# Scores and states of a pair in one TensorE run, fewer loads in flight, last rows in three parts: a retention layer with an MLP mixer

## The chip, the cores and the metric

The kernel runs on one core of a Trainium2 chip. The metric is the device time of one execution in microseconds (us); the time of a kernel is the median of its runs. Names in this text: PE is TensorE, PEld its weight loads, DVE is VectorE, ACT is ScalarE, POOL is GpSimd, SP is SyncE, whose queue issues most DMAs of the later part. A "line" such as L423 is a line of the kernel before, as the profile gives it.

## The reference

Four batches (B), eight heads (H), 768 steps (S), head width 64 (D). The first part is a recurrent retention layer, the second an MLP mixer over its output with 512 channels.

```python
def _attn_ref(q, k, v):
    gamma = 1.0 - 2.0 ** (-5.0 - np.arange(H))
    scale = 1.0 / np.sqrt(D)
    for t in range(S):
        state = gamma[None, :, None, None] * state + np.einsum('bhd,bhe->bhde', k[:, :, t], v[:, :, t])
        y[:, :, t] = scale * np.einsum('bhd,bhde->bhe', q[:, :, t], state)

def _moe_ref(x, w_tok1, w_tok2, w_ch1, w_ch2):      # x: (4, 768, 512), heads side by side
    xt = x.transpose(0, 2, 1)
    h = np.maximum(xt @ w_tok1, 0.0) @ w_tok2       # 768 -> 256 -> 768 along the steps
    u = x + h.transpose(0, 2, 1)
    h2 = np.maximum(u @ w_ch1, 0.0) @ w_ch2         # 512 -> 1536 -> 512 along the channels
    return u + h2
```

Inputs and output are float32; the kernel multiplies in 16-bit floats and adds up in float32.

## The kernel before

The retention layer is computed in six chunks of 128 steps. Two heads are handled together as a pair; a batch has four pairs, here written (b,p) for pair p of batch b. For each pair there is a **front**:

- q, k and v arrive by DMA. k is scaled into 16 bits on DVE (L332), q and v are cast: in batches 0 and 1 by the DMA itself, in batches 2 and 3 on POOL (L313).
- k and q are turned (head width onto partitions): on PE (L348, L352) with a copy out (L360) in batches 0 and 1, by a transposing DMA on SP's queue (L367) in batches 2 and 3.
- **states**: ten matmuls, 64 columns wide, k chunk by v chunk (L381). Each head uses 64 columns of the array. DVE adds the five products up with decay (U, L390 and L393), ACT and DVE write the result as r (L400, L407).
- **scores**: twelve matmuls on 64 rows of the array each (L423), in two halves of three chunks. DVE multiplies them by the causal mask (L436, "am", four a pair).
- **y**: q by state (L457) and masked scores by v (L460), two halves; ACT and DVE scale them into x (L471, L475), POOL casts x (L488).
- The token mixing: L510 (with w_tok1), a relu on ACT (L518), L531 (with w_tok2), an addition on DVE (L538), a cast of u on POOL (L549). u is turned on PE in batch 0 (L562, copied by ACT at L571) and by a transposing DMA in the other batches (L585; the variable `wide` chooses).

For each batch there is a **back**: the channel mixing, ch1 (L618, 384 columns, 96 matmuls a batch) with a relu on ACT (L631), and ch2 (L651, 512 columns, 72 a batch) with an addition on DVE (L660) and a store of 128 rows by SP (L667).

The program has a planner of its own, `arrange()`. Every operation is an `Op` with an engine, a time of occupation, a latency, dependencies and the tile slots that it takes. The planner places operations one by one on the engines by earliest start and priority, and the instructions are then issued in that order; each engine runs its own list strictly in order. Front matmuls go ahead of back matmuls (priority 0 and 1), back matmuls fill the time in between. `GUARD` is added to the planned start of a front matmul of batches 1 to 3, `SEM` stands for a semaphore, `RING` is the number of loads that the planner lets SP and POOL have in flight, `LATE` sets a pair's priority against the others. These numbers act on the order alone; the hardware waits for semaphores.

PSUM has eight banks: five "fa" (all fronts) and three "ba" (back; in batch 0 also the front). The banks of a name go round in order of taking. Before the change, states take one fa bank, each half of the scores two, and the three are separate operations on PE that the planner can put in different places. In batch 0 matmuls on zeros (L210) fill waits of PE.

Of the kernel before, what the change touches and what calls it, by code (L numbers as in the profile page):

```python
# [10 lines left out]
FP = mybir.dt.float32  # L11
# [6 lines left out]
def kernel(  # L18
# [11 lines left out]
    nc = tc.nc  # L30
    B, H, S, D = q.shape
    P = 128
    NC = S // P
    HC = NC // 2
    NP = H // 2
    C = H * D
# [45 lines left out]
    NR = 4  # L82
    r16 = [const_p.tile([P, NC - 1, P], F16, name=f"r16_{i}") for i in range(NR)]
    for t in r16:
# [7 lines left out]


    BUFS = dict(kf=4, qf=4, vf=4, k16=3, q16=4, v16=4, kT=4, qT=4, U=3, am=8, x16=2, h1=4, u16=3, u16w=2,
                x=3, uT=3, h2=2, o=3, r16=NR, fa=5, ba=3)
    SEM, GUARD = 80, 100
    EARLY, LATE, DIRECT = 1000, 12, 3
    LONG, XK, XQ, XU, XBAR = 1, 2, 2, 1, 1200
    RING = dict(SP=3, POOL=6)
    QLONG = 1200  # L100
    ASIDE, RACT = ((1, 1), (1, 3), (2, 1), (2, 3), (3, 1), (3, 3)), ()
    KPOOL = ()
    FREE, FILL, TOKBA, PRE, TWICE, SOFT = 4, 0.75, 2, 2, 1, 2
    ops = []

    class Slot:
# [97 lines left out]
    def tile_of(slot, pool, shape, dtype, tag=None):  # L204
        tag = tag or slot.tag
        slot.tile = pool.tile(shape, dtype, name=tag, bufs=BUFS[tag])
        if pool is ps:

            for _ in range(idle[0]):
                nc.tensor.matmul(slot.tile, zero[:, :P], zero, start=True, stop=True)  # L210
            idle[0] = 0
        return slot.tile
# [21 lines left out]
    def front(b, p):  # L234
# [6 lines left out]

        def op(eng, occ, lat, emit, deps=(), takes=(), uses=()):
            n[0] += 1
            pr = (0 if eng == "PE" else 1, b, n[0] + LATE * p, p)
            o = Op(eng, pr, occ, lat, emit, deps, takes, uses, guard=g if eng == "PE" else 0)
            o.first = p if first else None
            return o
# [79 lines left out]
        def emit():  # L327
            k16 = tile_of(K, sb, [P, NC, 2, D], F16)
            for j in range(2):
                h = 2 * p + j  # L330
                src = KF.tile[:, j * NC:(j + 1) * NC, :]
                (nc.gpsimd if keng == "POOL" else nc.vector).tensor_scalar(  # L332
                    k16[:, :, j, :], src, gk[:, h:h + 1], None, ALU.mult)
# [6 lines left out]
        def turn(src, dst, dep, eng):  # L340
            T = Slot(*FB)

            def emit():
                T.tile = tp = tile_of(T, ps, [P, 512], FP).bitcast(F16)
                for c in range(NC):
                    if src is Q and soft and b < LONG:
                        for j in range(2):
                            nc.tensor.transpose(tp[j * D:(j + 1) * D, c * P:(c + 1) * P],  # L348
                                                src.tile[:, j * NC + c], ident16)
                        continue  # L350
                    o = src.tile[:, c] if src is K else src.tile[:, 2 * c:2 * c + 2]
                    nc.tensor.transpose(tp[:, c * P:(c + 1) * P], o.rearrange("p h d -> p (h d)"), ident16)  # L352
            t = op("PE", 340, 500, emit, [dep, t1_done.get(b * NP - 1) if b > 0 else None], [T], [src])

            def emit():
                d, o = tile_of(dst, sb, [P, S], F16), T.tile[:, :S]
                if dst is QT and b < LONG:
                    d = d.rearrange("d (f p i) -> d f i p", f=2, i=HC)
                    o = o.rearrange("d (f i p) -> d f i p", f=2, i=HC)
                (nc.scalar.copy if eng == "ACT" else nc.vector.tensor_copy)(d, o)  # L360
            occ = dict(ACT=1350 if dst is QT and b < LONG else 700, DVE=470)[eng]
            return op(eng, occ, occ + 90, emit, [t], [dst], [T])
# [11 lines left out]

        ST, US, RS = Slot(*FB), Slot("U"), Slot("r16")

        def emit():
            st = tile_of(ST, ps, [P, 512], FP)
            for c in range(NC - 1):
                for j in range(2):  # L380
                    nc.tensor.matmul(st[j * D:(j + 1) * D, c * D:(c + 1) * D], K.tile[:, c, j],  # L381
                                     V.tile[:, j * NC + c], start=True, stop=True)
        pp = op("PE", 300, 470, emit, [kc, vc, y_done.get(b * NP + p - 2), t1_done.get(b * NP - 1) if b > 0 else None], [ST], [K, V])
        prev = None
        for c in range(NC - 1):
            def emit(c=c):
# [22 lines left out]

        AM = [Slot("am") for _ in range(4)]  # L410
        am_ops = []
        two_before = y_done.get(b * NP + p - 2)
        for hf in range(2):
            A = [Slot(*FB), Slot(*FB)]

            def emit(hf=hf, A=A):
                a = [tile_of(A[j], ps, [P, 512], FP).rearrange("p (i t) -> p i t", t=P)
                     for j in range(2)]
                for i in range(HC):
                    t = slice((hf * HC + i) * P, (hf * HC + i + 1) * P)  # L420
                    for j in range(2):
                        r = slice(j * D, (j + 1) * D)
                        nc.tensor.matmul(a[j][:, i], KT.tile[r, t], QT.tile[r, t],  # L423
                                         start=True, stop=True)
            a = op("PE", 180, 350, emit, [kt, qt, two_before], A, [KT, QT])
            for j in range(2):
                off = first and (p, 2 * hf + j) in ASIDE
                M = AM[2 * hf + j]

                def emit(j=j, A=A, off=off, M=M):  # L430
                    am = tile_of(M, sb, [P, HC, P], F16)
                    src = A[j].tile.rearrange("p (i t) -> p i t", t=P)
                    if off:
                        nc.scalar.copy(am, src[:, :HC])
                    else:
                        nc.vector.tensor_tensor(am, src[:, :HC], mask, ALU.mult)  # L436
                m = op(*(("ACT", 390, 470) if off else ("DVE", 470, 550)), emit, [a], [M], [A[j]])
                if off:
                    def emit(M=M):
                        nc.gpsimd.affine_select(  # L440
                            out=M.tile, in_=M.tile, compare_op=ALU.is_ge, fill=0.0,
                            base=0, pattern=[[0, HC], [1, P]], channel_multiplier=-1)
                    m = op("POOL", 470, 540, emit, [m], [], [M])
                am_ops.append(m)
# [73 lines left out]
            nc.scalar.activation(h1.rearrange("p j c -> p (j c)"), T1.tile[:, :NJ * P], AF.Relu)  # L518
        hr = op("ACT", 300, 380, emit, [t1], [H1], [T1])
        tt, uc = [], None  # L520
        wide = b >= XU
        T, UW = Slot(*FT), Slot("u16w")
        for hf in range(2):
            T2, U16 = Slot(*FT), UW if wide else Slot("u16")
# [73 lines left out]
    def back(b):  # L598
# [37 lines left out]
        def ch2(sh):  # L636
            H2, rel = halves[sh]
            for i in range(HC):

                parts = 2 if (b, sh, i) == (B - 1, 1, HC - 1) else 1  # L640
                CW = C // parts
                for part in range(parts):
                    A, O = Slot("ba"), Slot("o")
                    cs = slice(part * CW, (part + 1) * CW)
                    last = None
                    for f0 in range(0, NF, 2):
                        def emit(f0=f0, i=i, A=A, H2=H2, cs=cs, CW=CW):
                            if f0 == 0:
                                tile_of(A, ps, [P, 512], FP)
                            for ft in range(f0, f0 + 2):  # L650
                                nc.tensor.matmul(A.tile[:, :CW], H2.tile[:, ft, i * P:(i + 1) * P],  # L651
                                                 wc2[:, ft, cs],
                                                 start=(ft == 0), stop=(ft == NF - 1))
                        last = op("PE", 432 // parts, 432 // parts + 170, emit,
                                  rel[f0:f0 + 2] + [wops["c2", 0], last],
                                  [A] if f0 == 0 else [], [H2] if f0 == 0 else [A, H2])

                    def emit(sh=sh, i=i, A=A, O=O, cs=cs, CW=CW):
                        o = tile_of(O, sb, [P, C], FP)
                        nc.vector.tensor_tensor(o[:, :CW], X.tile[:, sh * HC + i, cs], A.tile[:, :CW],  # L660
                                                ALU.add)
                    ad = op("DVE", 80 + CW, 160 + CW, emit,
                            [last] + [x_add[b, p, sh] for p in range(NP)], [O], [A, X])

                    def emit(sh=sh, i=i, O=O, cs=cs, CW=CW):
                        t0 = (sh * HC + i) * P
                        nc.sync.dma_start(out=out[b, t0:t0 + P, cs], in_=O.tile[:, :CW])  # L667
                    st = op("SP", 100, 100, emit, [ad], [], [O])
                    st.prio, st.dma = (-2, b), 800 // parts

        for part in ((ch1, 0), (ch1, 1), (ch2, 0), (ch2, 1)) if b < TWICE else ((ch1, 0), (ch2, 0), (ch1, 1), (ch2, 1)):
            part[0](part[1])
# [52 lines left out]
```

## Time and profile before

| | us |
|---|---|
| median of 7 runs | 201.38 (201.27 to 201.99) |
| the profiled execution | 201.54 |
| its span | 199.8 |
| back matmuls, L618 busy | 69.5 |
| back matmuls, L651 busy | 68.0 |
| masks, L436 busy on DVE | 28.1 |
| relus of ch1, L631 busy on ACT | 46.4 |

The span runs from the first instruction to the last in the profile; the execution's time is a little longer. Matmuls are pipelined: one that is listed with 326 ns can start 163 ns after the one before it. So the distance between starts, not the listed length, tells what PE spends on a matmul. Idle time stands in square brackets behind an instruction, with what ended it.

### The profile page before, as it was taken

To read this page: it belongs to the slowest core of one execution; us is meant where nothing else is said; L and a number is where in the kernel's file an instruction comes from. 1 tells how busy PE (TensorE), PEld (TensorE's weight loads), DVE (VectorE), ACT (ScalarE), POOL (GpSimd) and SP (SyncE) were. 2 spreads that over 40 slices of the span, in tenths; PEclk is the share of its full clock that TensorE was granted. 3 is DMA by queue.
4 is the path that set the end of the run, shared out by engine and by line. 5 is a ranking of instruction groups with operands and counts; after the bars stand their busy time and mean duration, and the time that the engine had idled before them with its cause. 6 is when DMAs were issued, how large, how long until landed. Compare 5 with 4: busy or idle time off the path is not lost.

```text
span 199.8 us, 4681 instructions
## 1 busy us (share of the span) xinstructions
PE 190.2 (95%) x1868; PEld 116.4 (58%) x1868; DVE 112.7 (56%) x285; ACT 92.5 (46%) x207; POOL 76.7 (38%) x124
## 2 busy tenths in 40 slices
PE   7688899999999999999999999999999999999993
PEld 2444696667755664666566745675657545545552
DVE  6498965398568875683969376938481121021021
ACT  7259988886555200553226511563127405504600
POOL 7997999913901450235333504152422100000000
PEclk9999999999999999999999999999999999999999
DMA  6999999999998999999999999999940121012012
GB/s 113 178 216 186 208 228 199 160 190 218 155 95 187 202 246 164 223 250 158 206 204 239 234 171 242 235 206 194 185 122 27 39 86 72 3 52 105 0 52 105
DMA packets 90069, 31.75 MB, mean 159 GB/s; under 512 B 82592, under 2 KB 85920, under 8 KB 90048
## 3 DMA queue, kind: packets, MB, share of 16 engines
q1 hardware_dynamic: 64800, 21.63, 56.0%
q0 software_dynamic: 25248, 9.83, 40.3%
q8 instruction: 14, 0.23, 0.5%
q14 instruction: 7, 0.06, 0.1%
HBM read 26.74 MB, written 6.29 MB: 165 GB/s over the span
## 4 chain that ended last, share of the span: by engine, by line
PE 73%; DMA 10%; POOL 6%; issue 3%; ACT 2%; SPq 2%; DVE 2%; POOLq 0%
PE ba L618 30%; PE ba L651 25%; DMA kf<-in_k_dram 5%; PE fa L531 4%; PE fa L510 4%; DMA vf<-in_v_dram 3%; DMA qf<-in_q_dram 2%; PE fa L423 2%; SPq L367 2%; PE fa L460 2%; PE fa L381 1%; POOL v L301 1%; PE fa L457 1%; PE fa L352 1%; POOL v L313 1%
## 5 line engine op out<-in xcount | busy, mean ns | idle before, releaser
L618 PE MATMUL ba<-uT,wc 128*128 128x384 f16 x384 | 69.5, 326 | 0.0
L651 PE MATMUL ba<-wc,h 128*128 128x512 f16 (+1 forms) x300 | 68.0, 371 | 0.0
L631 ACT ACTIVATE h<-ba 128x384 f16<-128x384 f32 x96 | 46.4, 491 | 35.3 <-PE ba L618 34.5
L618 PEld LDWEIGHTS <-wc 128*128 128x128 f16 x384 | 35.6, 98 | 21.7
L651 PEld LDWEIGHTS <-h 128*128 128x128 f16 x300 | 27.5, 98 | 26.6
L660 DVE TENSOR_TENSOR o<-x,ba 128x512 f32<-128x512 f32 (+1 forms) x25 | 16.6, 665 | 38.6 <-PE ba L651 38.3
L436 DVE TENSOR_TENSOR am<-fa,mask 128x384 f16<-128x384 f32 x55 | 28.1, 550 | 4.1 <-PE fa L423 3.9
L488 POOL CAST x<-x 128x384 f16<-128x384 f32 x30 | 14.9, 509 | 31.2 <-issue 21.0
L538 DVE TENSOR_TENSOR x<-x,fa 128x384 f32<-128x384 f32 x31 | 16.1, 549 | 9.3 <-PE fa L531 8.8
L549 POOL CAST u16w<-x 128x384 f16<-128x384 f32 x24 | 12.0, 514 | 23.7 <-DVE x L538 22.8
L471 ACT ACTIVATE x<-fa,gy 128x192 f32<-128x192 f32 (+1 forms) x34 | 12.5, 422 | 17.7 <-PE fa L460 17.7
L332 DVE TENSOR_SCALAR k<-kf,gk 128x384 f16<-128x384 f32 x32 | 14.4, 493 | 5.4 <-DMA kf<-in_k_dram 5.4
L393 DVE SCALAR_TENSOR_TENSOR U<-U,gp,fa 128x64 f32<-128x64 f32 x56 | 15.5, 278 | 1.3
L518 ACT ACTIVATE h<-fa 128x256 f16<-128x256 f32 x15 | 5.7, 383 | 18.9 <-PE fa L510 15.7
L400 ACT ACTIVATE r<-U 64x320 f16<-64x320 f32 x16 | 7.5, 467 | 14.3 <-DVE U L393 14.2
L460 PEld LDWEIGHTS <-am 128*128 128x128 f16 x192 | 12.2, 98 | 2.2
L531 PE MATMUL fa<-h,wt 128*128 128x128 f16 x186 | 13.2, 219 | 0.0
L531 PEld LDWEIGHTS <-wt 128*128 128x128 f16 x192 | 11.9, 98 | 2.1
L510 PEld LDWEIGHTS <-wt 128*128 128x128 f16 x192 | 11.7, 98 | 2.0
L510 PE MATMUL fa<-x,wt 128*128 128x128 f16 x180 | 12.5, 219 | 0.0
L460 PE MATMUL fa<-v,am 128*128 128x64 f16 x174 | 12.5, 193 | 0.0
L313 POOL CAST q<-qf 128x768 f16<-128x768 f32 x8 | 6.6, 827 | 14.9 <-DMA qf<-in_q_dram 12.4
(74 smaller groups left out, 179.6 us busy)
## 6 DMA issues: line engine op xcount, KB each, us to landing
out_dram<-o SPq DMA_DIRECT2D x23, 256.0 KB, 2.5
kf<-in_k_dram SPq DMA_DIRECT2D x9, 384.0 KB, 5.0
qf<-in_q_dram SPq DMA_DIRECT2D x8, 384.0 KB, 5.0
vf<-in_v_dram SPq DMA_DIRECT2D x8, 384.0 KB, 5.6
kf<-in_k_dram POOLq DMA_DIRECT2D x7, 384.0 KB, 10.3
v<-in_v_dram POOLq DMA_DIRECT2D x8, 192.0 KB, 6.8
wc<-in_moe_w_ch_dram POOLq DMA_DIRECT2D x1, 1536.0 KB, 13.5
wc<-in_moe_w_ch_dram POOLq DMA_DIRECT2D x1, 1024.0 KB, 14.7
```

What stands on the lines that cost most here:

```text
L332: (nc.gpsimd if keng == "POOL" else nc.vector).tensor_scalar(k16[:, :, j, :], src, gk[:, h:h + 1], None, ALU.mult)
L393: nc.vector.scalar_tensor_tensor(U[:, c], U[:, c - 1], gp[:, p:p + 1], o, ALU.mult, ALU.add)
L436: nc.vector.tensor_tensor(am, src[:, :HC], mask, ALU.mult)
L460: nc.tensor.matmul(o[:, j * D:(j + 1) * D], AM[2 * hf + j].tile[:, i], V.tile[:, j * NC + c], start=(c == 0), stop=(c == 0 or j == 1))
L488: nc.gpsimd.tensor_copy(X16.tile[:, half(hf)], X.tile[:, half(hf), pc])
L510: nc.tensor.matmul(acc[:, jt * P:(jt + 1) * P], wt1[:, i, jt * P:(jt + 1) * P], X16.tile[:, i], start=(i == 0), stop=(i == NC - 1))
L531: nc.tensor.matmul(acc[:, i * P:(i + 1) * P], wt2[:, jt, t], H1.tile[:, jt], start=(jt == 0), stop=(jt == NJ - 1))
L538: nc.vector.tensor_tensor(xo, xo, T2.tile[:, :HC * P].rearrange("p (i d) -> p i d", d=P), ALU.add)
L618: nc.tensor.matmul(acc[:, :SH], w[:, ct, f * P:(f + 1) * P], UT.tile[:, ct, sh * SH:(sh + 1) * SH], start=(ct == 0), stop=(ct == NP - 1))
L631: nc.scalar.activation(H2.tile[:, ft], A.tile[:, :SH], AF.Relu)
L651: nc.tensor.matmul(A.tile[:, :CW], H2.tile[:, ft, i * P:(i + 1) * P], wc2[:, ft, cs], start=(ft == 0), stop=(ft == NF - 1))
L660: nc.vector.tensor_tensor(o[:, :CW], X.tile[:, sh * HC + i, cs], A.tile[:, :CW], ALU.add)
```

## The change

Part 1: for batches 1 to 3 (`WHOLE = 1`) the two halves of the scores and the states become one operation on PE, scores first; it takes all five fa banks. Batch 0 keeps the three operations.

Part 2: numbers of the planner. `GUARD` 100 to 150, `RING` of SP 3 to 2, `LATE` for batches 1 to 3 12 to 20, occupation times `AOCC` and `SOCC` for separate scores and states, and `LAG`: a run of batches 2 and 3 depends on the L510 of the second pair of the batch before, no longer of its last pair.

Part 3: u of pair (1,3) is turned on PE (`NOX`), not by a transposing DMA.

Part 4: output tiles 5 in place of 3; the last 128 rows are computed, added and stored in parts of 256, 192 and 64 columns in place of two of 256.

```diff
     BUFS = dict(kf=4, qf=4, vf=4, k16=3, q16=4, v16=4, kT=4, qT=4, U=3, am=8, x16=2, h1=4, u16=3, u16w=2,
-                x=3, uT=3, h2=2, o=3, r16=NR, fa=5, ba=3)
-    SEM, GUARD = 80, 100
+                x=3, uT=3, h2=2, o=5, r16=NR, fa=5, ba=3)
+    SEM, GUARD = 80, 150
...
-    RING = dict(SP=3, POOL=6)
+    RING = dict(SP=2, POOL=6)
...
+    WHOLE, AOCC, SOCC = 1, (370, 520), (360, 500)
+    NOX, LAG = ((1, 3),), 2
...
-            pr = (0 if eng == "PE" else 1, b, n[0] + LATE * p, p)
+            pr = (0 if eng == "PE" else 1, b, n[0] + (LATE if first else 20) * p, p)
...
-            t = op("PE", 340, 500, emit, [dep, t1_done.get(b * NP - 1) if b > 0 else None], [T], [src])
+            t = op("PE", 340, 500, emit, [dep, t1_done.get(b * NP - 1 - LAG * (b > 1)) if b > 0 else None], [T], [src])
...
+        A = [[Slot(*FB), Slot(*FB)] for _ in range(2)]
+        two_before = y_done.get(b * NP + p - 2)
+        whole = b >= WHOLE
...
+        def emit():
+            emit_a(0)
+            emit_a(1)
+            emit_st()
+
+        t1_last = t1_done.get(b * NP - 1 - LAG * (b > 1)) if b > 0 else None
+        if whole:
+            pp = op("PE", 790, 950, emit, [kt, qt, kc, vc, two_before, t1_last], A[0] + A[1] + [ST],
+                    [KT, QT, K, V])
+        else:
+            pp = op("PE", *((300, 470) if first else SOCC), emit_st, [kc, vc, two_before, t1_last], [ST], [K, V])
...
-            a = op("PE", 180, 350, emit, [kt, qt, two_before], A, [KT, QT])
+            a = pp if whole else op("PE", *((180, 350) if first else AOCC), lambda hf=hf: emit_a(hf), [kt, qt, two_before], A[hf], [KT, QT])
...
-        wide = b >= XU
+        wide = b >= XU and (b, p) not in NOX
...
-                parts = 2 if (b, sh, i) == (B - 1, 1, HC - 1) else 1
-                CW = C // parts
-                for part in range(parts):
+                parts = (256, 192, 64) if (b, sh, i) == (B - 1, 1, HC - 1) else (C,)
+                for part, CW in enumerate(parts):
...
-                    st.prio, st.dma = (-2, b), 800 // parts
+                    st.prio, st.dma = (-2, b), 800 * CW // C
```

`emit_a(hf)` and `emit_st()` are the bodies of the old operations: the six score matmuls of half `hf`, and the ten states matmuls.

In the built program this also reorders SP's queue. For batches 2 and 3 the order of loads and transposing DMAs was, in part, `uT(2,0) kT(2,2) qT(2,2) qf(2,3) vf(2,3)`, and later `uT(2,1) ... qT(2,3) kf(3,0) qf(3,0) ... vf(3,0) uT(2,2) kf(3,1) kT(3,0) qT(3,0)`. It becomes `kT(2,2) qT(2,2) qf(2,3) vf(2,3) uT(2,0)` and `qT(2,3) kf(3,0) qf(3,0) ... uT(2,1) kT(3,0) vf(3,0) qT(3,0) kf(3,1) qf(3,1) uT(2,2)` (kf, qf, vf: loads; kT, qT, uT: turned tiles).

More of the change, by code (lines that the diff above doesn't have):

```diff
@@ L375, in front, with emit_st @@
         ST, US, RS = Slot(*FB), Slot("U"), Slot("r16")
-        def emit():
+        A = [[Slot(*FB), Slot(*FB)] for _ in range(2)]
+        two_before = y_done.get(b * NP + p - 2)
+        whole = b >= WHOLE
+        def emit_st():
             st = tile_of(ST, ps, [P, 512], FP)
@@ L382, in emit, with emit_a @@
                                      V.tile[:, j * NC + c], start=True, stop=True)
-        pp = op("PE", 300, 470, emit, [kc, vc, y_done.get(b * NP + p - 2), t1_done.get(b * NP - 1) if b > 0 else None], [ST], [K, V])
+        def emit_a(hf):
+            a = [tile_of(A[hf][j], ps, [P, 512], FP).rearrange("p (i t) -> p i t", t=P)
+                 for j in range(2)]
+            for i in range(HC):
+                t = slice((hf * HC + i) * P, (hf * HC + i + 1) * P)
+                for j in range(2):
+                    r = slice(j * D, (j + 1) * D)
+                    nc.tensor.matmul(a[j][:, i], KT.tile[r, t], QT.tile[r, t], start=True, stop=True)
+        def emit():
[8 more added lines that the diff above has]
+            pp = op("PE", *((300, 470) if first else SOCC), emit_st, [kc, vc, two_before, t1_last], [ST], [K, V])
         prev = None
@@ L411, in front @@
         am_ops = []
-        two_before = y_done.get(b * NP + p - 2)
         for hf in range(2):
[L414 to L424, printed above, removed]
-            a = op("PE", 180, 350, emit, [kt, qt, two_before], A, [KT, QT])
+            a = pp if whole else op("PE", *((180, 350) if first else AOCC), lambda hf=hf: emit_a(hf), [kt, qt, two_before], A[hf], [KT, QT])
             for j in range(2):
@@ L428, in front, with emit @@
                 M = AM[2 * hf + j]
-                def emit(j=j, A=A, off=off, M=M):
+                def emit(j=j, A=A[hf], off=off, M=M):
                     am = tile_of(M, sb, [P, HC, P], F16)
@@ L436, in emit @@
                         nc.vector.tensor_tensor(am, src[:, :HC], mask, ALU.mult)
-                m = op(*(("ACT", 390, 470) if off else ("DVE", 470, 550)), emit, [a], [M], [A[j]])
+                m = op(*(("ACT", 390, 470) if off else ("DVE", 470, 550)), emit, [a], [M], [A[hf][j]])
                 if off:
@@ L638, in ch2 @@
             for i in range(HC):
-                parts = 2 if (b, sh, i) == (B - 1, 1, HC - 1) else 1
-                CW = C // parts
-                for part in range(parts):
+                parts = (256, 192, 64) if (b, sh, i) == (B - 1, 1, HC - 1) else (C,)
+                for part, CW in enumerate(parts):
                     A, O = Slot("ba"), Slot("o")
-                    cs = slice(part * CW, (part + 1) * CW)
+                    c0 = sum(parts[:part])
+                    cs = slice(c0, c0 + CW)
                     last = None
@@ L653, in emit @@
                                                  start=(ft == 0), stop=(ft == NF - 1))
-                        last = op("PE", 432 // parts, 432 // parts + 170, emit,
+                        last = op("PE", 432 * CW // C, 432 * CW // C + 170, emit,
                                   rel[f0:f0 + 2] + [wops["c2", 0], last],
```

## The prediction

> **What bounds the kernel now.** I read the page first: shares of the engines, the slices, the chain that ended last.
>
> ```profile
> PE 190.2 (95%) x1868; PEld 116.4 (58%) x1868; DVE 112.7 (56%) x285; ACT 92.5 (46%) x207; POOL 76.7 (38%) x124
> ...
> PE   7688899999999999999999999999999999999993
> ...
> PEclk9999999999999999999999999999999999999999
> DMA  6999999999998999999999999999940121012012
> ...
> PE 73%; DMA 10%; POOL 6%; issue 3%; ACT 2%; SPq 2%; DVE 2%; POOLq 0%
> ```
>
> TensorE (PE) is busy for 90% or more of every slice from the sixth to the last but one (a slice is 5.0 us), at full clock; no other engine is above 60%. The DMA row is full up to about 145 us, so late operands are the second possible bound. The profiled execution took 201.54 us, 1.74 us more than its span of 199.8, and 0.16 us more than the median of 201.38. I sum against 201.54 and take 0.16 off at the end.
>
> Next the chain in order of time gives the pitch of undisturbed matmuls:
>
> ```profile
> 157.66 7.77 PE ba L651 x36
> 165.43 7.80 PE ba L618 x48
> ```
>
> So 7.80/48 = 0.1625 us for a 384-column matmul and 7.77/36 = 0.216 us for a 512-column one (0.056 us for 128 columns, from 0.67 us for 12). Against these pitches the timeline of PE shows what the change is about (start, length, line):
>
> ```profile
> 37.45 0.98 PE L618 MATMUL ba<-uT,wc 128*128 128x384 f16 x5
> 38.35 0.35 PE L381 MATMUL fa<-v,k 128*64 128x64 f16 x10
> 38.63 0.50 PE L618 MATMUL ba<-uT,wc 128*128 128x384 f16 x2
> ```
> ```profile
> 39.88 0.51 PE L423 MATMUL fa<-qT,kT 64*128 64x128 f16 x12
> 40.32 0.99 PE L618 MATMUL ba<-uT,wc 128*128 128x384 f16 x5
> ```
>
> Lengths overlap, so starts are what counts. Five L618 matmuls should take 5 x 0.1625 = 0.81 us, but the states (L381) start 0.90 after the first: 0.09 for going in. The states hold PE 38.63 - 38.35 = 0.28. Seven L618 follow, 7 x 0.1625 = 1.14, and the scores (L423) start after 1.25: 0.01 for the first matmul after a small run (it shows 0.336 instead of 0.326) and 0.10 for going in. The scores hold PE 0.44. Where a pair's scores stand in two halves:
>
> ```profile
> 126.17 0.34 PE L423 MATMUL fa<-qT,kT 64*128 64x128 f16 x6
> 126.44 0.51 PE L531 MATMUL fa<-h,wt 128*128 128x128 f16 x6
> 126.88 0.34 PE L423 MATMUL fa<-qT,kT 64*128 64x128 f16 x6
> ```
>
> a half holds 0.27, so six matmuls cost 0.44 - 0.27 = 0.17 and going out 0.27 - 0.17 = 0.10. Such a transition is no idle time for the profile; it hides in "busy".
>
> Last the gaps behind which PE really waited:
>
> ```profile
> 86.75 0.35 PE L381 MATMUL fa<-v,k 128*64 128x64 f16 x10 [0.39 <-POOL v L313]
> 122.68 0.35 PE L381 MATMUL fa<-v,k 128*64 128x64 f16 x10 [0.27 <-POOL v L313]
> ```
>
> Going through all runs after 32 us by starts and pitches, six places are longer than pitch plus transitions: 81.7 (0.14), 86.7 (0.46), 92.5 (0.03), 101.6 (0.22), 117.7 (0.18), 122.7 (0.34): 1.36 us of waiting, most of it for the cast of v or a turned q. Everything else on PE after 32 us is work and transitions.
>
> **The change part by part.** I write (b,p) for pair p of batch b. In the changed program PE's order is the same up to the transposes of (1,0) at 37 us, so nothing moves before that.
>
> Scores and states in one run, 12 pairs. Before, an unsplit pair costs 0.09 + 0.28 + 0.01 + 0.10 + 0.44 + 0.01 = 0.93. After: 0.10 in, 0.44 scores, x for the seam from scores to states, 0.28 states, 0.01. The 0.44 already holds a going out of 0.10. This seam is not in the trace; its reverse is, in batch 0:
>
> ```profile
> 8.53 0.35 PE L381 MATMUL fa<-v,k 128*64 128x64 f16 x10 [1.07 <-DMA v<-in_v_dram]
> 8.80 0.34 PE L423 MATMUL fa<-qT,kT 64*128 64x128 f16 x6
> ```
>
> States straight before scores hold 0.27 to 0.28, as they do before a full-width matmul: one going out, no going in beside it. I take the same for the seam, x = 0: after = 0.83, saved 0.10 a pair, 1.20 for twelve. Bounds: nothing is drained (x = -0.10, 2.40 in all) and out plus in are both paid (x = +0.09, 0.12 in all). Three pairs, (1,1), (1,3), (3,1), stand in halves before; each pays one more in and out, 0.10 + 0.10 + 0.01, together 0.63. Sum: -1.83, between -0.75 and -3.03.
>
> The Trainium skill, "TensorEngine Tiling (Array Packing)", section Key Properties, says that changing the tiling mode, not just the tile, drains TensorE. Scores use 64-row, states 64-column tiles, so by that rule "unbroken" still holds one drain: it stands by x = 0, and against a reader's hope of x = -0.10, with which the total below would be 1.2 us lower.
>
> Edits that only steer the planner: AOCC and SOCC are read by no pair (batch 0 keeps the old numbers, all others are whole). GUARD 150 for 100, SP's ring of 2 for 3, 20 for LATE and LAG (the runs of batches 2 and 3 wait for the L510 of two pairs earlier than before) move work but add no instruction. Their price is what becomes of the 1.36 us of waits: from -1.36 (all gone) to the rival below. The six waits would each shrink by at most 0.05 through the larger guard, 0.3 in all; I take -0.15. Output tiles 5 for 3: nothing waited for them (VectorE's output additions, L660, waited for PE), cost 0.
>
> The run takes all five "fa" banks, so the next user (L510, L531 or y) waits for the first mask (L436). After the scores at 83.11 the first mask started at 83.48 and took 0.55: a bank is free 0.92 after the run's start. The nearest follower in the changed order is L510 of (2,0), 1.87 us behind the start of the run of (2,1): covered, price 0. Were VectorE just then in a k scaling (L332, 0.93 for two), the cover would be gone and cost 0 to 0.1.
>
> The u of (1,3) is turned on PE: six 128-column transposes, 6 x 0.056 = +0.34 us on the path. Its copy on ScalarE (700 ns class; L360's copy of the same 128x768 has a pitch of 0.70) lies beside PE; ScalarE is at 46%. If its cover went, ch1 of batch 1 would wait up to 0.7. One transposing DMA leaves SP's queue.
>
> Last rows in three parts: the 512 columns are the same, twelve more matmuls at about 0.0025 us of fixed time each (0.1625 - 384/2400) = +0.03. If a 64-column matmul cannot run under 0.038 (a y triple L457, L460, L460 takes 0.115 with three weight loads), +0.13. Behind the last matmul:
>
> ```profile
> 196.64 0.42 DVE L660 TENSOR_TENSOR o<-x,ba 128x256 f32<-128x256 f32 x1 [0.89 <-PE ba L651]
> ```
> ```profile
> out_dram<-o SPq DMA_DIRECT2D x1, 128.0 KB, 1.7
> ```
>
> The 512-column addition has a mean of 0.686, so a column costs (0.686 - 0.42)/256 = 1.0 ns and 64 columns take 0.42 - 0.20 = 0.22. But SP is now busy: the 192-column store is issued 0.36 + 0.05 after its matmuls, which end 12 x 0.029 = 0.35 before the last; two SP issues stood at least 0.47 apart (60.45, 60.92). So the last issue comes at 0.41 + 0.47 - 0.35 = 0.53 after the last matmul, against 0.49 now. Landing: 2.0 for 256 KB, 1.7 for 128 KB, so 32 KB gains at most 0.22. Net -0.1, from -0.2 to +0.2.
>
> "DMA: Bandwidth & Descriptors", section Specifications, gives 512 B as the smallest transfer at line rate and a read-modify-write below; 64 columns are rows of 256 B. No store here shows it; by that rule the last landing gains nothing and the sum is about 0.1 higher.
>
> Sum: -1.83 - 0.15 + 0.34 + 0.03 - 0.10 = -1.71. 201.54 - 1.71 = 199.83, less 0.16: **199.7 us**.
>
> **Rivals.**
>
> Late operands (slower). A run now needs k, v, both turned tiles and all five "fa" banks at once, and PE is in order: all matmuls behind it wait, and with them ScalarE's relus, y, and the stores on SP. Adding the pitches along the changed PE order, the runs of batches 2 and 3 are due at 77.4, 85.8, 93.8, 102.9, 111.5, 124.9, 136.6, 141.3 us. The turned q landed before at 76.4, 82.9, 96.5, 106.1, 117.6, 124.3, 135.6, 145.5. Four would be late, (3,0) by 6.1 us. For a better landing speaks SP's new order: the turned k and q of (2,2) go ahead of uT of (2,0), which had held SP 2.8 us at 88.7; the turned k and q of (3,0) go ahead of uT of (2,2), which held it 2.65 us at 107.8, and of the next k load, and uT of (2,1) (1.25 us) goes behind the loads of (3,0). Taking just these 2.65 + 1.25 off, q of (3,0) lands at 113.7, 2.2 us late. Price 2.2: 199.7 + 2.2 = 201.9. It decides from 1.7 us of added waiting, a landing after 113.2. Against it: v and the turned tiles were at most 0.46 us late before though the DMA row was full, and the new order moves back-half matmuls ahead of the runs as it needs. (3,1) is tightest on VectorE: 4.6 us from run to y, for four masks at a pitch of 0.47, five U steps of 0.3, one r of 0.51: 3.9.
>
> Both drains paid, that is, the run is not unbroken for PE: -0.75 - 0.15 + 0.27 = -0.63, 200.8. For it: shapes differ on both sides of the seam. Against it: the reverse seam paid one.
>
> No drain at the seam: 1.2 more, 198.5. Against it: states before scores held as long as before L618.
>
> **How the numbers follow.** Forecast 0.54 (199.0 to 200.6), no drain 0.12, both drains 0.12, late operands 0.22. A measurement of this kernel can tell about 0.2%, 0.4 us, from no change. Below 200.98 lie the forecast but for 0.03, no drain and half of both drains: 0.54 - 0.03 + 0.12 + 0.06 = 0.69, rounded with the low end of late operands to 0.70. Above 201.78 lies most of late operands, 0.20, same is 0.10. Range 198.2 (no drain and 0.3 less waiting) to 202.0.
>
> **What would show it.** In the profile of the changed kernel: scores to states 0.44 (forecast), 0.34 (no drain) or 0.53 (both); 0.28 from the first states matmul to the next; PE waits after 32 us of some 1.2 us in sum; the last store issued about 0.5 us after the last matmul. Wrong, if a run at 94, 103, 112 or 141 us stands behind a gap released by a turned tile or by L313, or if y (L457, L460) waits for VectorE.

## The result and the profile after

The changed kernel took 200.11 us in the median of 27 runs, the kernel before 201.30 us in 64 runs beside it: ratio 0.9933, 95% interval 0.9917 to 0.9949. That is 1.35 us less at 201.3, against a forecast of 1.7. The ratio is taken without the few executions in a slower state, so it is not the quotient of the two medians, 0.9941. Single runs reach from 198.23 to 201.97, so only ratios with their intervals are compared below.

The profiled execution took 200.47 us (its span is 198.8), 1.07 less than the profiled execution before. Its page (shares of the engines, the slices of PE and DMA, the chain that ended last):

```profile
PE 189.4 (95%) x1886; PEld 117.4 (59%) x1886; DVE 108.9 (55%) x286; ACT 93.6 (47%) x208; POOL 77.2 (39%) x124
...
PE   7887999999999999999996999999999999999993
...
DMA  6999999999599999999998999999921131012013
...
PE 75%; DMA 10%; POOL 4%; DVE 3%; SPq 2%; ACT 2%; issue 1%; POOLq 0%; DVEq 0%
```

The picture is the same, PE at 95%, but the 22nd slice of PE (104.4 to 109.3 us) is now at 6 tenths. All waits of PE after 32 us that the view of waits names:

```profile
PE fa L524 <- DVE am L450: 1.5, 1, 1.5
PE fa L387 <- DVE x L489: 0.3, 1, 0.3
```

(Engine, line and releaser: total us, times, longest. Line numbers of the changed kernel: scores L397, states L387, masks L450, k scaling L334, scaling of y L489, the two matmuls of the token mixing L524 and L545, ch1 L632, ch2 L665.) The two waits for the cast of v that this view named before (0.39 and 0.27) are gone.

The first unbroken run, in the timeline of PE (start, length):

```profile
38.61 0.81 PE L632 MATMUL ba<-uT,wc 128*128 128x384 f16 x4
39.36 0.51 PE L397 MATMUL fa<-qT,kT 64*128 64x128 f16 x12
39.80 0.35 PE L387 MATMUL fa<-v,k 128*64 128x64 f16 x10
40.08 0.82 PE L632 MATMUL ba<-uT,wc 128*128 128x384 f16 x4
```

Four ch1 matmuls should take 0.65 and the scores start after 0.75: 0.10 for going in. Scores to states 0.44, states to ch1 0.28. Scores held 0.44 before a full-width matmul too, so the seam costs one going out and saves one going in, x = 0 of the prediction. All twelve runs read so, between 0.438 and 0.439, but for one that waits inside (0.80, below). The drain that the Trainium skill, "TensorEngine Tiling (Array Packing)", section Key Properties, states for a change of mode fits this direction as well: 0.44 in place of 0.34.

The hole in it, first on PE, then on VectorE, where the cause is to be seen:

```profile
103.12 0.51 PE L397 MATMUL fa<-qT,kT 64*128 64x128 f16 x12
103.56 0.35 PE L387 MATMUL fa<-v,k 128*64 128x64 f16 x10
103.84 1.47 PE L632 MATMUL ba<-uT,wc 128*128 128x384 f16 x8
106.84 0.27 PE L524 MATMUL fa<-x,wt 128*128 128x128 f16 x2 [1.53 <-DVE am L450]
```

```profile
105.35 0.75 DVE L334 TENSOR_SCALAR k<-kf,gk 128x384 f16<-128x384 f32 x2 [2.86 <-DMA kf<-in_k_dram]
106.01 0.22 DVE L416 COPY U<-fa 128x64 f32<-128x64 f32 x1
106.15 0.55 DVE L450 TENSOR_TENSOR am<-fa,mask 128x384 f16<-128x384 f32 x1
```

The run of (2,3) is done at 103.8 and its masks could start. But VectorE's list has the k scaling of (3,0) ahead of them, and that waits until 105.35 for its load (landed at 105.32). The run holds all five fa banks, the first mask frees the first of them, and L524 of (2,2) needs it: PE stands for 1.53 us, 1.69 by pitch. The wait of 0.29 (0.36 by pitch) inside the run of (2,1) at 86 is the same thing: there the k scaling of (2,2), waiting for its load until 85.20, stood ahead of the scaling of y (L489) that frees a bank.

```profile
85.20 0.75 DVE L334 TENSOR_SCALAR k<-kf,gk 128x384 f16<-128x384 f32 x2 [3.12 <-DMA kf<-in_k_dram]
85.86 0.55 DVE L489 TENSOR_TENSOR x<-fa,gyw 128x384 f32<-128x384 f32 x1
```

By pitch, the waits after 32 us are 1.69, 0.36 and a third of 0.19 before y at 64.27, which waits for a mask on VectorE and shows as 0.03 of idle time only.

By the ruler of the prediction (starts against pitches and transitions), in us:

| | before | after |
|---|---|---|
| start of the first ch1 matmul (end of the first stage) | 32.22 | 31.92 |
| transitions into and out of scores and states | 1.90 more | 0 (taken as base) |
| waits of PE after 32 us | 1.35 | 2.24 |
| end of the last matmul to landing of the last store | 2.18 | 2.08 |
| span | 199.8 | 198.8 |

The sum: -0.30 (first stage) - 1.90 + 0.34 + 0.03 (forecast terms of PE) + 0.89 (waits) - 0.10 = -1.04, measured -1.06. These are two single executions. Without the first stage, whose instructions the change does not touch, they differ by 0.76 us, where the medians differ by 1.35.

### The profile page after: what moved, and what is told of

Same layout as the page of the kernel before. It is cut to its first block, busy times and chain, and to the rows that moved or that the text cites. A ratio compares the mean times of both kernels' runs of the same rounds, so it can differ in the third digit from the quotient of the medians.

```text
span 198.8 us, 4714 instructions
## 1 busy us (share of the span) xinstructions
PE 189.4 (95%) x1886; PEld 117.4 (59%) x1886; DVE 108.9 (55%) x286; ACT 93.6 (47%) x208; POOL 77.2 (39%) x124
## 4 chain that ended last, share of the span: by engine, by line
PE 75%; DMA 10%; POOL 4%; DVE 3%; SPq 2%; ACT 2%; issue 1%; POOLq 0%; DVEq 0%
PE ba L665 30%; PE ba L632 26%; DMA kf<-in_k_dram 10%; PE fa L545 5%; PE fa L524 5%; PE fa L397 2%; PE fa L474 2%; SPq L369 2%; PE fa L471 1%; POOL v L303 1%; PE fa L387 1%; PE fa L354 1%; DVE k L334 1%; POOL kf L278 1%; POOL q L300 1%
## 5 line engine op out<-in xcount | busy, mean ns | idle before, releaser
L632 PE MATMUL ba<-uT,wc 128*128 128x384 f16 x384 | 68.0, 326 | 0.0
L665 PE MATMUL ba<-wc,h 128*128 128x512 f16 (+3 forms) x312 | 67.8, 363 | 0.0
L632 PEld LDWEIGHTS <-wc 128*128 128x128 f16 x384 | 36.1, 98 | 22.1
L665 PEld LDWEIGHTS <-h 128*128 128x128 f16 x312 | 28.1, 98 | 25.9
L674 DVE TENSOR_TENSOR o<-x,ba 128x512 f32<-128x512 f32 (+3 forms) x26 | 16.8, 645 | 36.1 <-PE ba L665 33.8
L450 DVE TENSOR_TENSOR am<-fa,mask 128x384 f16<-128x384 f32 x55 | 30.2, 550 | 0.1
L334 DVE TENSOR_SCALAR k<-kf,gk 128x384 f16<-128x384 f32 x32 | 14.3, 488 | 13.6 <-DMA kf<-in_k_dram 13.6
L563 POOL CAST u16w<-x 128x384 f16<-128x384 f32 x22 | 11.0, 522 | 13.1 <-DVE x L552 13.1
L524 PEld LDWEIGHTS <-wt 128*128 128x128 f16 x192 | 11.8, 98 | 4.1 <-issue 1.9
L524 PE MATMUL fa<-x,wt 128*128 128x128 f16 x180 | 12.5, 219 | 1.5 <-DVE am L450 1.5
L545 PEld LDWEIGHTS <-wt 128*128 128x128 f16 x192 | 11.8, 98 | 2.1
L545 PE MATMUL fa<-h,wt 128*128 128x128 f16 x186 | 13.0, 219 | 0.0
L315 POOL CAST v<-vf 128x768 f16<-128x768 f32 x8 | 6.6, 827 | 15.2 <-DMA vf<-in_v_dram 15.2
L474 PE MATMUL fa<-v,am 128*128 128x64 f16 x174 | 11.9, 193 | 0.0
```

The costliest lines, as they stand in the source:

```text
L334: (nc.gpsimd if keng == "POOL" else nc.vector).tensor_scalar(k16[:, :, j, :], src, gk[:, h:h + 1], None, ALU.mult)
L474: nc.tensor.matmul(o[:, j * D:(j + 1) * D], AM[2 * hf + j].tile[:, i], V.tile[:, j * NC + c], start=(c == 0), stop=(c == 0 or j == 1))
L524: nc.tensor.matmul(acc[:, jt * P:(jt + 1) * P], wt1[:, i, jt * P:(jt + 1) * P], X16.tile[:, i], start=(i == 0), stop=(i == NC - 1))
L545: nc.tensor.matmul(acc[:, i * P:(i + 1) * P], wt2[:, jt, t], H1.tile[:, jt], start=(jt == 0), stop=(jt == NJ - 1))
L632: nc.tensor.matmul(acc[:, :SH], w[:, ct, f * P:(f + 1) * P], UT.tile[:, ct, sh * SH:(sh + 1) * SH], start=(ct == 0), stop=(ct == NP - 1))
```

## The experiments

Waits are PE's after 32 us in the one profiled execution, by starts and pitches (matmuls at a lower clock, in e3, count in them); ratios are to the kernel before, on the same chip. Runs that insert lines have their line numbers shifted by one to four: L524 of the changed kernel is L527 in f1 and L528 in g1.

| run | what | ratio, 95% interval | waits, us | first ch1 at, us |
|---|---|---|---|---|
| e1_k_behind | two k scalings later on VectorE | 0.9926 (0.9900 to 0.9953) | 2.6 | 30.84 |
| e2_seam_broken | one matmul in the seam | 0.9967 (0.9942 to 0.9991) | 0.3 | 31.89 |
| e3_run_alone | the run, nothing else | 1.0124 (1.0099 to 1.0150) | 6.6 | 30.89 |
| e4_run_undone | all but the run | 1.0116 (1.0094 to 1.0138) | 2.3 | 32.31 |
| f1_wide_loads | rows of 1536 B in the loads | 0.9850 (0.9815 to 0.9884) | 0.3 | 31.66 |
| f2_no_nox | u of (1,3) by DMA | 1.0022 (0.9988 to 1.0057) | 2.9 | 30.88 |
| f3_two_parts | last rows in two parts | 0.9962 (0.9935 to 0.9989) | 1.6 | 31.88 |
| f4_ring3 | three loads in flight | 1.0068 (1.0043 to 1.0094) | 3.6 | 31.90 |
| g1_k30_behind | one k scaling later | 0.9928 (0.9889 to 0.9967) | 2.3 | 30.81 |
| g2_nox_two | u of (2,0) on PE too | 0.9975 (0.9947 to 1.0003) | 1.7 | 31.56 |
| g3_guard100 | guard 100 | 1.0047 (1.0019 to 1.0075) | 4.2 | 30.85 |
| g4_lag0 | no LAG | 0.9922 (0.9888 to 0.9956) | 1.9 | 32.32 |

**e2: is the seam worth what it seems?** In the changed kernel:

```diff
             st = tile_of(ST, ps, [P, 512], FP)
+            if whole:
+                nc.tensor.matmul(st[:, :P], zero[:, :P], zero[:, :P], start=True, stop=True)
```

> The changed kernel with one more matmul on zeros (128x128, 0.056 us) between the scores and the states of each of the twelve pairs, in the bank of the states, which then overwrite it. Nothing else moves. Theory A (the seam saves one going in): scores to states grows from 0.44 to 0.59, 12 x 0.15 = 1.8 us in all, of which waits that stand behind it may swallow up to half; time 0.9 to 1.8 us above the changed kernel. Theory B (the seam is worth nothing): 12 x 0.056 = 0.7 us or less.

Its timeline of PE at one run:

```profile
77.73 0.51 PE L399 MATMUL fa<-qT,kT 64*128 64x128 f16 x12
78.18 0.23 PE L386 MATMUL fa<-zero 128*128 128x128 f16 x1
78.34 0.35 PE L389 MATMUL fa<-v,k 128*64 128x64 f16 x10
```

Scores to states is 0.60 (the rows round) in place of 0.44: the matmul of 0.056 and one more going in of 0.10, some 1.9 us for twelve pairs, as theory A has it. The time rose by 0.0034 of 201.3, 0.7 us: under theory A's range and at the bound of theory B, and the intervals of the two ratios overlap by a hair. So the trace shows what the seam saves on PE, and the time does not tell the two theories apart. Where the rest may have gone shows in the waits of the profiled execution: 0.3 us, against 2.24 in the changed kernel, though both first stages ended at 31.9. A slower PE met its operands later and waited less. So PE time saved in this stage seems to be worth only a part of itself.

**f1: what sets the waits?** In the changed kernel, for SP's loads of batches 2 and 3:

```diff
+                    if b >= SOFT:
+                        return eng.dma_start(out=t.rearrange("p (h c) d -> p h (c d)", h=2),
+                                             in_=rows.rearrange("h (p c) d -> p h (c d)", p=P))
                     dma = eng.dma_start(out=t, in_=rows.rearrange("h (c p) d -> p (h c) d", p=P))
```

> The changed kernel, but SP's loads of q, k and v in batches 2 and 3 put six steps in a row on each partition, in rows of 1536 B, where the kernel takes rows of 256 B; the same bytes, the same tiles, the same order everywhere. The steps of batches 2 and 3 so lie on other partitions than the masks and decays suppose, and the output is not the reference's. Theory A (what remains of waits is set by the landing of the loads, which hardly move when PE is faster): loads land earlier, k of (3,0) before 103 in place of 105.3, waits of PE after 32 us fall from 2.3 to under 0.8 us, ratio to the kernel before 0.980 to 0.988. Theory B (the order of the lists sets the waits, loads land when they are issued): landings move by less than 0.5 us, ratio 0.991 to 0.995.

The view of DMA for 60 to 142 us, first of the changed kernel, then of this one:

```profile
DMA packets 56500, 17.03 MB, mean 208 GB/s; under 512 B 54955, under 2 KB 54955, under 8 KB 56491
...
q1 hardware_dynamic: 56491, 16.90, 112.9%
```

```profile
DMA packets 26966, 17.77 MB, mean 217 GB/s; under 512 B 19020, under 2 KB 25164, under 8 KB 26956
...
q1 hardware_dynamic: 26956, 17.63, 95.2%
```

Half the packets for about as many bytes. k of (3,0) landed at 102.05 in place of 105.32, the last load (v of (3,3)) at 133.72 in place of 138.97. And the place of the hole:

```profile
103.10 0.35 PE L390 MATMUL fa<-v,k 128*64 128x64 f16 x10
103.38 1.47 PE L635 MATMUL ba<-uT,wc 128*128 128x384 f16 x8
104.69 0.83 PE L527 MATMUL fa<-x,wt 128*128 128x128 f16 x12
```

L527 follows its eight ch1 matmuls without a gap; no wait of PE is left in the view of waits. The same lists on all engines, 0.985: theory A. What waits the changed kernel has left are set by when the loads land. The layout itself is no improvement that could be kept, since chunks of 128 steps are needed on the partitions.

**e1 and g1: is it the place of the k scaling?** VectorE's list is changed after planning, all other lists stay as they are:

```diff
+    MOVES = ((("k", 3, 0), ("am", 2, 3, 1)), (("k", 2, 2), ("x", 2, 0, 1)))
...
+    for what, behind in MOVES:
+        mine = row[named[what].eng]
+        mine.remove(named[what])
+        mine.insert(mine.index(named[behind]) + 1, named[what])
```

g1 has the first of the two moves alone.

> The changed kernel with two rows of VectorE's list moved and nothing else: the k scaling of (3,0) goes behind the second mask of (2,3), that of (2,2) one place back, behind the scaling of y of (2,0). Theory A (the 1.69 us wait of L524 at 105.0 and the 0.36 us wait inside the run at 86 come from a k scaling that waits for its load at the head of VectorE's list and keeps masks and evacuations, and so fa banks, behind it): both waits fall under 0.3 in sum, the time is 1.3 to 1.8 us below the changed kernel, ratio to the kernel before about 0.986. Theory B (the loads are the bound, and PE meets the same delay one step later, at the run of (3,0)): the wait moves to the run near 112 and the time stays within 0.4 us of the changed kernel, ratio 0.992 to 0.995.

> The changed kernel with one row of VectorE's list moved: the k scaling of (3,0) behind the second mask of (2,3); that of (2,2) stays where it is. Theory A (the wait of 1.7 us at 105 was caused by that row and is a real loss): no wait behind masks near 105, ratio 0.985 to 0.989. Theory B (loads set the pace, a wait taken away there comes back before the run of (3,0) or later): no wait near 105 either, but 0.5 us or more of it comes back at a later place, ratio 0.990 to 0.994.

In both, the wait at 105 is gone, and in e1 that inside the run of (2,1) too: the mechanism is shown. But other waits came in their place. g1, waits of PE, then VectorE and POOL before the longest of them:

```profile
PE fa L528 <- POOL x L505: 0.9, 1, 0.9
PE fa L399 <- DMA qT<-q: 0.5, 1, 0.5
PE fa L389 <- DVE x L492: 0.2, 1, 0.2
```

```profile
120.22 1.20 DVE L335 TENSOR_SCALAR k<-kf,gk 128x384 f16<-128x384 f32 x2 [1.39 <-DMA kf<-in_k_dram]
121.34 0.54 DVE L492 TENSOR_TENSOR x<-fa,gyw 128x384 f32<-128x384 f32 x1
```

```profile
121.95 0.51 POOL L505 CAST x<-x 128x384 f16<-128x384 f32 x1 [0.74 <-DVE x L492]
```

The run of (3,0) now comes before its turned q. And at 121 the next k scaling waits for its load at the head of VectorE's list, with the scaling of y (L492) behind it; POOL's cast of x, which L528 needs, waits for that. It is the same mechanism on the same engine, with another pair's load; e1 and f2 show the same chain there. Both ratios lie in theory B's range and are not told apart from the changed kernel; e1's interval leaves theory A's 0.986 out, g1's just touches 0.989. One reservation: the profiled executions of e1 and g1 had a first stage 1.1 us shorter than that of the changed kernel, which brings PE to its operands sooner and makes waits by itself. So that waits came back is shown, but not how much of them the shorter first stage caused.

**e3 and e4: the run or the planner's numbers?** e3 sets all of the change but the run back (`GUARD` 100, `RING` 3, `LATE` 12, no `NOX`, `LAG` 0, three output tiles, two last parts); e4 takes the run back alone; its separate scores and states are planned with the new times (370 and 360 ns for 180 and 300 before), so its plan is not the old one with other numbers alone:

```diff
-    WHOLE, AOCC, SOCC = 1, (370, 520), (360, 500)
+    WHOLE, AOCC, SOCC = 4, (370, 520), (360, 500)
```

> The kernel before with the unbroken run alone: planner numbers, the transposing DMA of (1,3), output tiles and last parts as before. Theory A (the run is the gain): transitions as in the changed kernel, 1.8 us less PE time than before, waits somewhere between 0.5 and 3 us against 1.4: 199 to 201.5, ratio 0.99 to 1.00. Theory B (the planner's numbers are the gain): no gain, ratio 1.00 or above, with the transitions gone all the same and waits of 3 us or more.

> The changed kernel without the unbroken run (scores in two halves and states as operations of their own in all batches, with the new occupation times 370 and 360). Theory A: transitions of 1.2 us (unsplit) to 3 us (all split) come back, waits near 1.4: 201 to 203, ratio 1.00 to 1.01. Theory B (the planner's numbers are the gain): ratio 0.995 or lower.

Neither is faster than before; each is 1.2% slower, e4 a little above the range that theory A gave. Theory A was wrong on e3 and theory B on e4: neither part is the gain by itself. The run alone has the transitions of the changed kernel, but 6.6 us of waits (last figure of the row: PE idle before, and for what):

```profile
81.02 0.51 PE L397 MATMUL fa<-qT,kT 64*128 64x128 f16 x12 [2.08 <-DMA qT<-q]
81.46 0.35 PE L387 MATMUL fa<-v,k 128*64 128x64 f16 x10
82.72 0.29 PE L474 MATMUL fa<-v,am 128*128 128x64 f16 x2 [0.91 <-DVE am L450]
```

It needs k, q, v of (2,0) at once, the turned q is 2 us late, y waits next, and some 2.8 us of the 6.6 are matmuls at half clock behind it (last section). Without these 2.8 us e3 would stand near the kernel before, not below it. Without the run, seventeen score runs in place of twelve and the separate states bring 2.3 us of transitions back, and v is late three times (1.4 us in the view of waits). So in these plans the gain belongs to the two together: the run saves PE time, the numbers keep its operands from being late.

**f4, g3, f2, g4, g2: which of the numbers?** One number each, planned anew: `RING` of SP 3; `GUARD` 100; `NOX` empty; `LAG` 0; `NOX` with (2,0) too.

> The changed kernel with three row loads in flight on SP's ring in the plan; the lists behind 60 us are planned anew. Theory A (loads set the pace and any plan meets the same landings): landings of the loads of batches 2 and 3 within 1.5 us of the changed kernel's, waits 1 to 3 us, ratio 0.990 to 1.000. Rival (the ring number itself is the gain, since it puts turned tiles ahead of loads): turned tiles land 2 us and more later, waits of 4 us or more, ratio above 1.005.

> The changed kernel with the planner's guard at 100 as before. If the guard's 50 ns a front matmul is what keeps runs from standing early: waits 3 to 5 us against 2.3, ratio 1.000 to 1.010. If it is of no matter: 0.991 to 0.996.

> The changed kernel with u of (1,3) turned by the transposing DMA again; the planner plans anew, so the lists behind move a little. If DMA is short (theory A), 0.34 us less on PE is more than eaten by one more transposing DMA (1.2 us in SP's queue): ratio 0.993 to 1.000. If PE alone is the bound, 0.34 us faster than the changed kernel: 0.991 or less.

> The changed kernel with the runs of batches 2 and 3 bound to the last L510 of the batch before, as before. That binds two runs, (2,0) and (3,0), later than in the changed kernel. Since the operands of (3,0) land near 111 anyway, theory: ratio 0.991 to 0.997. Rival (the earlier run of (3,0) is a gain): 1.000 or more.

> The changed kernel with u of (2,0) turned on PE too, planned anew: 0.34 us more on PE, one transposing DMA less among the loads of 75 to 100 us. If the loads set the pace: loads of batch 3 land 0.5 to 1.5 us earlier, ratio 0.986 to 0.993. If a new plan costs more than a transposing DMA is worth: ratio 0.995 or more.

The ring at 3 gave 3.6 us of waits, the guard at 100 gave 4.2. f4's loads landed as in the changed kernel up to k of (2,2) (85.42 and 85.17), then sooner, k of (3,0) by 6 us (99.36), and yet it was slower. One wait is for ACT's copy of the u turned on PE (0.9 us), as ch1 stands right behind the transposes in PE's list. Another, 0.9 inside the run of (2,1), is the k scaling of (2,2) again: it stood at the head of VectorE's list for 3.80 us, and the scaling of y behind it. Neither expectation held whole. g3's waits, 4.2 us as expected, are for late operands by the names in the view:

```profile
PE fa L397 <- DMA kT<-k: 1.3, 1, 1.3
PE fa L397 <- DMA qT<-q: 1.0, 1, 1.0
PE fa L576 <- POOL v L315: 0.9, 1, 0.9
PE ba L632 <- DMA uT<-u16w: 0.5, 1, 0.5
```

Without the transposes on PE (f2), 0.34 us of PE work goes and the time rises by 0.9%: ch1 of batch 1 waits 0.8 us for the tile turned by DMA, and a turned q is late (0.6). That is part of it only: in the profiled execution PE's waits are 0.6 longer than in the changed kernel and its work 0.34 shorter, together 0.3 us. That execution, 200.41, is among the quicker half of the twelve, and six lie at 202.0 and above; what made those slow is not shown. A second pair turned on PE (g2) gains nothing more: 0.9975, with waits of 1.7, as the second expectation had it. `LAG` makes no difference (0.9922, the changed kernel 0.9933). As each of these plans moves hundreds of rows, they say what one number is worth in this plan, not by which row.

**f3: the last rows.** `parts = (256, 256)` in place of `(256, 192, 64)`; nothing else moves.

> The changed kernel with the last rows in two parts of 256 columns; no other row moves. The prediction's terms: PE 0.03 less, the tail behind the last matmul 0.1 more (3.1 to 3.4 us from the end of the last matmul to the end of the span): 0.1 us slower than the changed kernel, ratio 0.9935 to 0.995. Rival (the 256-byte rows of the 64-column part cost a slow store): equal or 0.2 faster.

From the end of the last matmul to the last landing 2.18 us, in the changed kernel 2.08, before 2.18. The ratio, 0.9962, lies above the expected range, but the times do not tell 0.1 us apart (0.9962 and 0.9933, intervals overlap). The store of 64 columns, in the view of DMA of the changed kernel after 196.3 us (median us to landing last):

```profile
out_dram<-o SPq DMA_DIRECT2D x1, 32.0 KB, 1.5
```

Its 32 KB in rows of 256 B landed 0.17 sooner after the issue than 128 KB in rows of 1 KB (1.70). So a penalty of short rows that eats up the gain of a smaller store does not show at this size.

No version tried that computes the layer beats the changed kernel by more than the intervals.

## Why the prediction was right, and where it was off

The forecast was 199.7 with 198.2 to 202.0; measured 200.11. The mechanism on PE was right; that the sum came so close owes something to luck, as the term of the waits shows. By its steps:

- Transitions, -1.83: right. 1.90 by the same ruler, with x = 0 at the seam as taken from the reverse seam of batch 0. "No drain" and "both drains" are out: 0.44 where 0.34 or 0.53 would have shown.
- Last rows, -0.10 and +0.03: right. The last issue came 0.56 after the last matmul (forecast 0.53), the landing gained 0.17. The 0.47 between two issues on SP was not the least, as the prediction read it: the next one at 60.92 was followed after 0.43. At the end it was 0.48.
- u of (1,3) on PE, +0.34: the PE cost is right, the value is not. The prediction gave nothing for the transposing DMA that leaves the queue; in f2, where it stays with the DMA and the plan is made anew, the time is 0.9% longer.
- Waits, -0.15: the term that was mis-sized. They grew by 0.89 in the profiled execution, 2.24 in all where some 1.2 was forecast. The step that failed is the one on the banks, "covered, price 0. Were VectorE just then in a k scaling ... cost 0 to 0.1". It priced the k scaling by its busy time. An instruction at the head of an in-order list holds up for as long as its own operand is late: 2.86 us here, 1.69 of which reached PE. How large this is in other executions is open: with the other terms as measured, the 1.35 us between the medians would leave waits only some 0.3 longer than before (an estimate, with first stages taken as alike: 1.90 + 0.10 - 0.34 - 0.03 - 1.35).
- The first stage ended 0.30 sooner, which the prediction did not have; its instructions are the same, so this is no part of the change; in the profiled execution it made up for a part of the waits.
- The rival of late operands was half right. Late operands are what ate into the gain, but not at the place that it named: no run stood behind a gap released by a turned tile or a cast, and of the signs named beforehand only a wait of y for VectorE came, 0.19 at 64.27; the turned q of (3,0) landed at 111.9, not 113.7, and what was late was that pair's k load, by way of VectorE's list and a bank.
- "At most 0.3" for the larger guard was far too small: at 100 the same kernel is 1.1% slower.

Where the saved PE time went, e2 and f1 show together, f1 more firmly: put 1.9 us back on PE and the waits of the profiled execution fall by as much (the time of e2 rose by 0.7 all the same); make the loads land sooner and the waits go with the PE time still saved.

## What to carry to other kernels

Before a saving on the busiest engine is counted in full, look at what sets the arrival of its operands: with transfers full over the same stage, a shorter engine turns part of the saving into waits. Price a wait in an in-order list by the lateness of what its first instruction waits for, never by that instruction's length; a load-fed instruction ahead of one that frees a buffer is the thing to look for. And fused runs that take every buffer of a pool make all others wait for the first release, so the fusion and the schedule around it have to be tuned together.

## What the runs showed of the hardware

The first stage has the same instructions in all fourteen traces, yet its end, the start of the first ch1 matmul, lay between 30.81 and 32.32 us. That is as much as the whole gain of the change, and may be a part of why single runs differ by 3 us; what sets it is not shown.

In e3, PE stood for 2.08 us at 79 to 81, worked for some 0.8, and stood for 0.91 again. Stretch by stretch (busy us of each engine, then the granted clock, DMA share, GB/s):

```profile
78.00:81.00 3.00, 0.94 (x6) 0.37 (x5) 2.75 (x9) 0.47 (x1) 0.00 (x0) 1.00 1.01 194
81.00:82.00 1.00, 0.79 (x22) 0.59 (x22) 0.15 (x1) 0.00 (x0) 0.00 (x0) 0.97 1.08 244
82.00:84.00 2.00, 1.28 (x12) 0.94 (x13) 1.97 (x7) 0.52 (x2) 0.00 (x0) 0.50 1.15 245
84.00:86.00 2.00, 2.00 (x15) 1.27 (x14) 1.88 (x5) 1.86 (x5) 1.01 (x2) 0.50 1.37 221
86.00:88.00 2.00, 2.00 (x11) 1.22 (x10) 0.90 (x3) 0.92 (x3) 0.91 (x2) 0.50 1.39 218
88.00:89.00 1.00, 1.00 (x11) 0.92 (x9) 0.00 (x0) 0.15 (x2) 0.81 (x1) 0.62 1.39 218
```

The clock was one half from 81.9 to 88.8 us, nearly 7 us; twelve matmuls of 128 columns then took 1.28 us (87.39 to 88.67) in place of 0.67. It fell when the second gap was 0.1 us old, so what stands ahead of the fall is one gap of 2.08 us and 0.8 us of work. The Trainium skill, "TensorE: Matmul & The Clock Gate", section "Why this matters for your kernels", advises against idle gaps over some 3 us; here the clock fell after a shorter one. That the gap was the cause is likely, but was not tested. In all six executions of e3 the mean granted clock was low, 0.981 to 0.992. A wait of 1.5 us, as in the changed kernel, left the clock at 1.0.
